# Hedgehog attention and a ReGLU feed-forward on one core: k and v of every batch in pairs of heads, a third output buffer, and a new order of work

## The chip, the cores and the metric

The kernel runs on one core of one Trainium2 chip. A core has a matrix engine (PE), whose weight loads are recorded apart (PEld); a vector engine (DVE); a scalar engine (ACT), which has the exponential; a general engine (POOL); and DMA engines, which take their work from queues that SP, POOL and ACT issue. Sums of PE land in eight PSUM banks of 128 x 512 words of 32 bits. The metric is the device time of one execution in microseconds, lower being better. The kernel before took 384.98 us (median of three runs: 384.98, 382.41 and 385.39).

## The reference

Attention with a feature map in place of the softmax (8 batches, 8 heads, 576 tokens, 64 dimensions, 128 features with both signs), whose output is laid out by token and fed to a gated feed-forward layer (4608 tokens, 512 wide, 1536 inside):

```python
def phi(x):                                   # x: (8, 8, 576, 64); w_phi: (64, 128)
    proj = np.einsum('bhsd,df->bhsf', x, w_phi)
    proj = proj - np.max(np.abs(proj), axis=-1, keepdims=True)
    return np.concatenate([np.exp(proj), np.exp(-proj)], axis=-1)
q_p, k_p = phi(q), phi(k)
kv  = np.einsum('bhsf,bhsd->bhfd', k_p, v)
z   = np.sum(k_p, axis=2)
num = np.einsum('bhsf,bhfd->bhsd', q_p, kv)
den = np.einsum('bhsf,bhf->bhs', q_p, z)[..., None] + 1e-06
x   = (num / den).transpose(0, 2, 1, 3).reshape(8 * 576, 512)
out = np.maximum(x @ w_gate, 0.0) * (x @ w_val) @ w_out
```

As written, `proj - max` is exponentiated with both signs, and the maximum is one number per token. The kernel therefore exponentiates the projection without it (exp(p) and exp(-p)) and brings exp(-max) and exp(max) in later, as factors of each token: on v for k (`ek`), and on the product for q (`cq`).

## The kernel before

**Atoms and their order.** The work of all eight batches is cut into some 1,400 pieces, the atoms. Each is a small function that issues a few instructions. They are registered in the order in which the program defines them, and they are run in the order of a string of numbers, `ORDER` (line 26). Nothing else sets the order: every engine, and every DMA queue, takes its instructions in the order in which the atoms issue them. A prime behind a number lets the atom choose the second of two engines (`copy_of`, for instance ACT in place of DVE for a copy). `zN` stands for filler: N matmuls of 512 columns on a tile of zeros, whose result nobody reads (`keep_busy`).

**Keys.** `kr` projects k with `w2` (w_phi twice, once in each half of the rows) in 64-row matmuls: the upper and lower half of PE's rows work on different heads or blocks, into two banks. For that k must stand with its 64 dimensions on the partitions. In batches 0 and 1 PE itself transposes k and q, and DVE or ACT copies the result out of PSUM (`tT`, `turned_copy`, line 284). From batch 2 on (`TURN = 2`) a transposing DMA on SP's queue does it (kT and qT, line 292). Then DVE takes the row maximum (line 319), ACT the two exponentials (`kp`, line 368) and the factors `ek`. POOL multiplies v by `ek` for both signs (`vs`, line 328), and the column behind them, a copy of `ek`, gives z.

**kv.** In batches 0 and 1, k and v are laid out in pairs of heads: the two heads of a pair have 2 x 576 tokens, laid on 128 partitions by 9, which makes 36 blocks of 128 rows for a batch, 64 rows of one head above 64 of the other. The blocks are worked in five or six items (`K_CUTS`), and `kv_pairs` (line 493) sums each half of the heads in 72 matmuls of 64 rows into two banks. Batches 2 to 7 take 512 tokens of each head in four blocks of 128 (four items of 8 blocks, one for each pair of heads), and the remaining 64 tokens of each head, the tails, in an item of their own for two batches at once: loads `km` and `vm`, a transposing DMA, a projection, and `vsm` (line 395), whose other half of the rows is zero. `kv_heads` (line 469) sums a pair of heads in 20 matmuls of 128 rows, 16 for the main tokens and 4 for the half-empty tails.

**Queries and the feed-forward.** q is projected in the same way, exponentiated on ACT (`qp`, line 565), and multiplied by kv (`n`, line 595). DVE puts the two signs together and divides (POOL or DVE for the last product, `xu`), and a DMA or PE transposes the result into `xT`, the input of the feed-forward layer. Its matmuls (`fv` and `fg`, line 725, four of 128 rows each; `fo`, line 773, twelve for a tile of 128 tokens) make the greater part of PE's work, and they are strewn between the small pieces of later batches' attention. A copy takes val out of PSUM (line 740), DVE makes h of it and the gate (line 747), a copy takes the output tile into one of two buffers `out_sb` (line 787), and a DMA on SP's queue stores it (line 754).

**Queues.** SP's queue carries v, the transposes and the stores; POOL's carries k, q and the weights, cast to bf16 on the way. A store that is issued behind a transpose waits for it on the queue.

## Time and profile before

| | |
|---|---|
| runs, us | 384.98, 382.41, 385.39 (median 384.98) |
| the profiled execution, us | 382.8, with a span of 380.8 |
| granted clock of PE | 1.00 |
| PE busy | 365.3 us, 96% of the span, 3452 matmuls |
| DVE, ACT, POOL busy | 290.4, 213.6, 151.2 us |
| feed-forward matmuls (lines 725 and 773) | 97.9 + 98.0 + 97.6 us of PE |
| kv in 128-row matmuls (line 486) | 480 |
| products of tails on POOL (line 395) | 12.3 us in 12 |
| stores of output | 32 of 256 KB, 2.9 us to landing |

The span runs from the first to the last recorded instruction; the time of the execution has 2.0 us around it. A group's row names the line, the engine and the operation, the tile written and those read, the shapes and the count; behind the bar stand its busy time and the mean of one, and behind the second bar the idle time of the engine ahead of these instructions, with what ended it. In a timeline row stand the start, the duration and the engine; brackets behind it hold a wait and what it waited for. A share of the chain that ended last says how much of the span had its cause on that engine or line.

### The profile page before, as it was taken

How to read it: one execution, taken by the hardware profiler on the slowest of the kernel's cores; microseconds unless marked ns; L12 is line 12 of the kernel's file. 1: busy time of each engine (PE TensorE's matmuls, PEld its weight loads, DVE VectorE, ACT ScalarE, POOL GpSimd, SP SyncE). 2: the span in 40 equal slices, each digit the busy share in tenths (PEclk: the TensorE clock that was granted, in tenths of full speed). 3: DMA queues.
4: the chain of work that ended last, by engine and by line, in shares of the span. 5: the costliest groups of instructions: out<-in, count | busy, mean ns of one | idle time of the engine just before them, and what ended most of it. 6: DMA issues, size and time to landing. Idle time of an engine off the chain costs nothing.

```text
span 380.8 us, 8916 instructions
## 1 busy us (share of the span) xinstructions
PE 365.3 (96%) x3452; PEld 196.8 (52%) x3502; DVE 290.4 (76%) x633; ACT 213.6 (56%) x509; POOL 151.2 (40%) x201
## 2 busy tenths in 40 slices
PE   7789999898999999999989999999999999999996
PEld 4467455445555545464545544465455444444443
DVE  6998989797886789888858886988768927834641
ACT  6997888776776556885864549882750212111101
POOL 5882663359265283911752035933710220010000
PEclk9999999999999999999999999999999999999999
DMA  8999999999199959880378768720410131011003
GB/s 258 204 200 218 228 143 143 199 239 118 36 208 228 161 87 167 164 183 14 72 126 197 108 162 126 144 16 16 109 58 2 28 87 53 3 53 71 2 0 110
DMA packets 87929, 45.10 MB, mean 118 GB/s; under 512 B 55824, under 2 KB 82000, under 8 KB 87888
## 3 DMA queue, kind: packets, MB, share of 16 engines
q1 hardware_dynamic: 60208, 30.42, 36.4%
q0 software_dynamic: 27200, 13.57, 28.2%
q10 hardware_dynamic: 480, 0.56, 0.5%
q8 instruction: 27, 0.44, 0.5%
q14 instruction: 14, 0.11, 0.1%
HBM read 37.78 MB, written 9.44 MB: 124 GB/s over the span
## 4 chain that ended last, share of the span: by engine, by line
PE 79%; ACT 8%; DMA 5%; POOL 2%; issue 2%; DVE 1%; SPq 1%; another core or an unknown queue 0%; DVEq 0%; POOLq 0%
PE pa L725 44%; PE pa L773 20%; PE pa L595 4%; PE pa L312 4%; PE pa L486 3%; ACT kp L368 3%; ACT qp L565 3%; DMA vn<-in_v_dram 3%; DMA out_dram<-out_sb 2%; PE pa L547 2%; POOL vs L328 1%; SPq L292 1%; PE pa L509 1%; PE pa L271 1%; DMA vn<-in_k_dram 1%
## 5 line engine op out<-in xcount | busy, mean ns | idle before, releaser
L725 PE MATMUL pa<-xT,wv_sb 128*128 128x512 bf16 (+1 forms) x384 | 97.9, 370 | 0.9
L725 PE MATMUL pa<-xT,wg_sb 128*128 128x512 bf16 (+1 forms) x385 | 98.0, 370 | 0.8
L773 PE MATMUL pa<-wo_sb,h 128*128 128x512 bf16 (+2 forms) x427 | 97.6, 373 | 1.1 <-issue 0.3
L747 DVE SCALAR_TENSOR_TENSOR h<-pa,val_sb 128x512 bf16<-128x512 f32 (+1 forms) x112 | 74.6, 669 | 26.8 <-PE pa L725 20.7
L740 ACT CAST val_sb<-pa 128x512 bf16<-128x512 f32 (+1 forms) x67 | 38.1, 575 | 97.9 <-PE pa L725 88.8
L635 POOL TENSOR_TENSOR xu<-u,r 128x512 bf16<-128x512 f32 x36 | 37.3, 1041 | 139.3 <-DVE r L633 69.7
L565 ACT ACTIVATE qp<-pa 128x512 bf16<-128x512 f32 x144 | 76.2, 616 | 14.4 <-PE pa L547 14.1
L368 ACT ACTIVATE kp<-pa 128x512 bf16<-128x512 f32 (+1 forms) x152 | 77.6, 603 | 11.8 <-PE pa L312 10.4
L328 POOL TENSOR_TENSOR vs<-vn,ek 128x512 bf16<-128x512 f32 (+1 forms) x68 | 67.4, 1004 | 34.4 <-DMA vn<-in_v_dram 18.0
L725 PEld LDWEIGHTS <-wv_sb 128*128 128x128 bf16 x448 | 41.8, 98 | 45.0 <-issue 1.2
L725 PEld LDWEIGHTS <-wg_sb 128*128 128x128 bf16 x448 | 41.6, 98 | 43.4 <-issue 0.5
L773 PEld LDWEIGHTS <-h 128*128 128x128 bf16 x444 | 40.8, 98 | 44.6 <-issue 0.8
L319 DVE TENSOR_REDUCE mq<-pa 128x4 f32<-128x512 f32 x72 | 46.5, 683 | 11.1 <-PE pa L312 11.0
L319 DVE TENSOR_REDUCE mk<-pa 128x4 f32<-128x512 f32 (+1 forms) x76 | 47.8, 654 | 3.9 <-ACT kp L368 2.3
L626 DVE TENSOR_TENSOR u<-pa,t 128x195 f32<-128x195 f32 (+3 forms) x120 | 38.1, 333 | 3.3
L614 DVE TENSOR_TENSOR t<-pa,cq 128x195 f32<-128x195 f32 (+3 forms) x120 | 36.9, 326 | 2.5 <-PE pa L595 1.3
L787 DVE COPY out_sb<-pa 128x512 f32<-128x512 f32 x21 | 14.5, 688 | 28.8 <-PE pa L773 20.3
L595 PEld LDWEIGHTS <-qp 128*128 128x128 bf16 x640 | 28.1, 98 | 14.2 <-ACT qp L565 0.9
L740 DVE CAST val_sb<-pa 128x512 bf16<-128x512 f32 (+1 forms) x45 | 30.7, 682 | 4.4 <-PE pa L725 3.0
L595 PE MATMUL pa<-kv,qp 128*128 128x65 bf16 x640 | 31.1, 193 | 1.1 <-ACT qp L565 0.5
L787 ACT COPY out_sb<-pa 128x512 f32<-128x512 f32 (+1 forms) x15 | 8.9, 594 | 23.5 <-PE pa L773 18.7
L486 PEld LDWEIGHTS <-kp 128*128 128x128 bf16 x480 | 16.7, 97 | 5.9 <-issue 1.5
(68 smaller groups left out, 262.7 us busy)
## 6 DMA issues: line engine op xcount, KB each, us to landing
out_dram<-out_sb SPq DMA_DIRECT2D x32, 256.0 KB, 2.9
vn<-in_v_dram SPq DMA_DIRECT2D x6, 1024.0 KB, 7.1
qn<-in_q_dram POOLq DMA_DIRECT2D x8, 512.0 KB, 8.5
kn<-in_k_dram POOLq DMA_DIRECT2D x6, 512.0 KB, 8.6
wv_sb<-in_moe_w_val_dram POOLq DMA_DIRECT2D x3, 512.0 KB, 10.4
wg_sb<-in_moe_w_gate_dram POOLq DMA_DIRECT2D x3, 512.0 KB, 9.1
wo_sb<-in_moe_w_out_dram POOLq DMA_DIRECT2D x1, 1536.0 KB, 19.9
vn<-in_v_dram SPq DMA_DIRECT2D x1, 1152.0 KB, 11.7
```

The lines of the kernel that those rows point to most:

```text
L319: nc.vector.tensor_reduce(m, some.rearrange("p (c f) -> p c f", f=F), axis=AX.X, op=ALU.max, apply_absolute_value=True,)
L328: eng.tensor_tensor(dst[:, :, s, 0:D], src, ek[:, :, s : s + 1].to_broadcast(list(src.shape)), op=ALU.mult,)
L368: nc.scalar.activation(st["kp"][:, s, 0 : n // 2, par, :], st["banks"][par][:, 0 : n // 2 * F].rearrange("p (a f) -> p a f", f=F), AF.Exp, ...
L565: nc.scalar.activation(x["qp"][:, s, slot].rearrange("p a b -> p (a b)"), st["cols", i][par], AF.Exp, scale=sign,)
L595: nc.tensor.matmul(pn[:, E * (2 * i + s) : E * (2 * i + s + 1)], lhsT=x["qp"][:, s, slot, blk, :], rhs=kv_of(b, lo + i)[:, s, :],)
L614: nc.vector.tensor_tensor(x["t", j][rows, 0:n], ab[:, :, 1], c[:, :, None].to_broadcast([np_, n, E]), op=ALU.mult,)
L626: nc.vector.tensor_tensor(x["u"][rows, lo : lo + n], ab[:, :, 0], x["t", j][rows, 0:n], op=ALU.add)
L635: copy_of(alt, nc.gpsimd, nc.vector).tensor_tensor(x["xu"], x["u"][:, :, 0:D], x["r"].to_broadcast([P, H, D]), op=ALU.mult)
L725: nc.tensor.matmul(ps, lhsT=w[:, dc, P * fi : P * fi + P], rhs=xTs[g][:, dc, lo:hi], start=(dc == 0), stop=(dc == NDC - 1),)
L740: copy_by(copy_of(alt, "ACT", "DVE"))(st["val", n], ps)
L747: nc.vector.scalar_tensor_tensor(st["h2"][:, fi, lo:hi], ps, 0.0, st["val", n], op0=ALU.max, op1=ALU.mult)
L773: nc.tensor.matmul(po, lhsT=st["h2"][:, fi, P * t : P * t + P], rhs=wo_sb[:, fi, c0:c1], start=(fi == 0), stop=(fi == NFC - 1),)
```

## The change

Batches 2 to 7 take the layout of batches 0 and 1. `load_k` and `load_v` call `load_pairs` for every batch; the transposing DMA of k covers 18 slices of 128 in place of 16, those of the tails go, and so do the loads `km` and `vm`, `k_tails`, `vsm`, the zeroed `vs_mix` and `kv_heads`. Every batch from 1 on has five items of k, of 8, 8, 8, 8 and 4 blocks, and two calls of `kv_pairs`. In numbers: PE does 1152 kv matmuls of 64 rows where it did 480 of 128 rows and 288 of 64. The exponentials of k go from 136 of 512 columns and 16 of 256 to 124 and 40. The pool of `kp` and `vs` has six buffers (five before, with the tails in another pool). `out_sb` has three buffers in place of two. `keep_busy` counts in halves: `z8` is four matmuls of 512 columns, `z1` one of 256; fillers are 15 of 512 and three of 256 columns where there were six of 512. The numbers of the atoms are others, so `ORDER` is another string throughout.

```diff
-ORDER = """7 z3 82 92 93 83' 84 87 94 86 8 0 98 102 85 89 90 91 88 103 z1 104 96 97 108 105 95 107 106 z1 112
+ORDER = """7 z8 49 59 60' 50 z1 51 53 61 63 55 8 64 1 52 0 69 70' z3 71 62 66 68 54 72 56 57' 58 z8 79 75 74
...
-    sb_k = ctx.enter_context(tc.tile_pool(name="sb_k", bufs=5))
+    sb_k = ctx.enter_context(tc.tile_pool(name="sb_k", bufs=6))
...
-    vs_mix = [singles.tile([P, H, 2, E], BF16, name=f"vsm{half}") for half in range(2)]
 
     def keep_busy(n):
-        scratch = bank()
-        for _ in range(n):
+        scratch = bank().rearrange("p (a b) -> p a b", b=P)
+        for i in range(0, n, 2):
+            wide = 2 * min(2, n - i)
             nc.tensor.matmul(
-                scratch.rearrange("p (a b) -> p a b", b=P),
+                scratch[:, 0:wide],
                 lhsT=zeros,
-                rhs=zeros[:, None, :].to_broadcast([P, 4, P]),
+                rhs=zeros[:, None, :].to_broadcast([P, wide, P]),
             )
...
     def load_k(b):
-        (load_pairs if b < TURN else load_main)(b, "kn", k, nc.gpsimd, BF16)
+        load_pairs(b, "kn", k, nc.gpsimd, BF16)
 
     def load_v(b):
-        (load_pairs if b < TURN else load_main)(b, "vn", v, nc.sync, FP32, buf=f"vn{b % 2}")
+        load_pairs(b, "vn", v, nc.sync, FP32, buf=f"vn{b % 2}")
...
     for i in range(B // 2):
-        if 2 * i >= TURN:
-            atoms.add("ld", f"km{i}")(lambda alt, i=i: load_tails(i, "km", k, nc.gpsimd, BF16))
-            atoms.add("ld", f"vm{i}")(lambda alt, i=i: load_tails(i, "vm", v, nc.sync, FP32))
...
-                t = inputs[f"{n}T", b] = sb_in.tile([P, H * C // 2, P], BF16, name=f"{n}T{b % 2}")
-                nc.sync.dma_start_transpose(
-                    out=t, in_=inputs[f"{n}n", b].rearrange("p h c d -> p (h c d)")
-                )
+                rows = inputs[f"{n}n", b]
+                if n == "q":
+                    rows = rows.rearrange("p h c d -> p (h c d)")
+                t = sb_in.tile([P, rows.shape[1] // P, P], BF16, name=f"{n}T{b % 2}")
+                inputs[f"{n}T", b] = t
+                nc.sync.dma_start_transpose(out=t, in_=rows)
...
-    for i in range(TURN // 2, B // 2):
-        atoms.add("turn", "km", i)(lambda alt, i=i: turn_tails("km", i))
...
-        if b >= TURN:
-            for u in range(NU):
-                st = k_item(
...
-                kv_heads(b, u, st)
-            return
-        cuts = [0] + K_CUTS[b] + [NB]
+        cuts = [0] + K_CUTS[min(b, 1)] + [NB]
...
-                None,
+                lambda lo=lo, hi=hi: inputs["kT", b][:, lo // 2 : hi // 2],
                 lambda lo=lo, hi=hi: v_blocks(lo, hi),
...
-                            out_sb = sb_g.tile([P, DM], FP32, name="out_sb", bufs=2)
+                            out_sb = sb_g.tile([P, DM], FP32, name="out_sb", bufs=3)
...
-    for half in range(2):
-        nc.vector.memset(vs_mix[half][SM * (1 - half) : SM * (2 - half)], 0.0)
```

Three places show how the instructions move. The lines of the changed kernel are some 60 to 80 lower where the same code stands further up (486 and 509 become 447, 754 becomes 690, 284 becomes 279).

The first is PE at the first kv block of batch 2. A row has the line, the operation, the tile written, and the tiles read; a number behind a name tells one buffer's use from the next, `kp` and `vs` are the exponentials of k and the scaled v of an item, `vsm0` the tails of v, and `pa` a PSUM bank. Before:

```order
L595 LDWEIGHTS qp_1526
L595 MATMUL pa_2019<-kv_1210,qp_1526 128x65
L486 LDWEIGHTS kp_1835
L486 MATMUL pa_2031<-vs_1832,kp_1835 128x65
...
L486 LDWEIGHTS kp_1681
L486 MATMUL pa_2031<-vsm0_102,kp_1681 128x65
```

and in the changed kernel:

```order
L307 LDWEIGHTS kT1_1566
L307 MATMUL pa_2027<-w2_100,kT1_1566 128x128
L447 LDWEIGHTS kp_1656
L447 MATMUL pa_2037<-vs_1791,kp_1656 128x65
L447 LDWEIGHTS kp_1656
L447 MATMUL pa_2038<-vs_1791,kp_1656 128x65
```

Before, 20 matmuls into one bank stand behind a 128-row product of q (line 595) and end with a tail's product after every four blocks. Now 72 matmuls into two banks in turn stand behind 64-row projections (line 307), and they need three items of the batch at once.

The second is ACT in the start, from the projections of the first queries to the first copies of val. `tT` is a transposed k or q, `xT` the input of the feed-forward layer, `x2` two such rows in a row. Before:

```order
L565 ACTIVATE qp<-pa 128x512 x2
L284 COPY tT_742<-pa 128x1024
L655 COPY xT<-pa 128x4x128 x2
L284 COPY tT_794<-pa 128x512
L368 ACTIVATE kp<-pa 128x4x128 x2
L740 CAST val_sb<-pa 128x256 x2
L655 COPY xT<-pa 128x4x128
```

and in the changed kernel:

```order
L503 ACTIVATE qp<-pa 128x512 x6
L279 COPY tT_756<-pa 128x512
L279 COPY tT_758<-pa 128x1024
L593 COPY xT<-pa 128x4x128
L279 COPY tT_794<-pa 128x1024
L363 ACTIVATE kp<-pa 128x4x128 x2
L676 CAST val_sb<-pa 128x256 x2
```

ACT has another copy of `tT` ahead of the first copy of `xT`, and the second copy of `xT` has gone to DVE.

The third is SP's queue at the end of batch 1 and the start of batch 2. A store's `out_sb` has the number of its buffer's use, `vn0` is v of batch 2, and the numbers behind `kT` and `qT` tell the batch's parity. Before:

```order
L292 DMA_TRANSPOSE qT0_1390<-qn_1388 128x16x128
L754 DMA out_0_dram<-out_sb_1484 128x512
L754 DMA out_0_dram<-out_sb_1596 128x512
L292 DMA_TRANSPOSE kT1_1607<-kn_1503 128x16x128
L214 DMA vn0_1635<-in_v_dram 128x8x256
L754 DMA out_0_dram<-out_sb_1668 128x512
L236 DMA vm_1685<-in_v_dram 64x8x64 x2
L298 DMA_TRANSPOSE qmT_1713<-qm_1710 128x4x128
L754 DMA out_0_dram<-out_sb_1776 128x512
```

and in the changed kernel:

```order
L291 DMA_TRANSPOSE qT0_1225<-qn_945 128x16x128
L690 DMA out_0_dram<-out_sb_1528 128x512
L218 DMA vn0_1536<-in_v_dram 128x4x576
L291 DMA_TRANSPOSE kT1_1566<-kn_1564 128x18x128
L690 DMA out_0_dram<-out_sb_1606 128x512
L690 DMA out_0_dram<-out_sb_1672 128x512
L690 DMA out_0_dram<-out_sb_1734 128x512
L295 DMA_TRANSPOSE qmT_1768<-qm_1740 128x4x128
```

The load of v has moved from behind the transpose of k3 and behind the second store to the place directly behind the first store. Three stores stand behind the transpose where there were two, and the tails' loads are gone.

151 lines of the change are left out of this document (55 added, 96 removed), and 33 rows, old and new, of the table ORDER.

## The prediction

> **What bounds the kernel now.** I read the page first, then the table of windows, then the chain.
>
> ```profile
> span 380.8 us, 8916 instructions
> PE 365.3 (96%) x3452; PEld 196.8 (52%) x3502; DVE 290.4 (76%) x633; ACT 213.6 (56%) x509; POOL 151.2 (40%) x201
> ...
> PE 79%; ACT 8%; DMA 5%; POOL 2%; issue 2%; DVE 1%; SPq 1%; another core or an unknown queue 0%; DVEq 0%; POOLq 0%
> ```
>
> PE is busy 96% of the span and makes 79% of the chain that ended last. Such a share is an average, so the next view asks where the other 15.5 us lie. Its columns are the stretch, its length, and the busy time (and count) of PE, PEld, DVE, ACT and POOL, then clock and DMA.
>
> ```profile
> 0.00:10.00 10.00, 7.82 (x37) 4.03 (x37) 6.43 (x13) 6.64 (x20) 5.06 (x14) 1.00 0.84 254
> 10.00:20.00 10.00, 7.70 (x160) 5.11 (x159) 9.78 (x20) 9.88 (x32) 9.04 (x14) 1.00 1.28 205
> 20.00:30.00 10.00, 8.55 (x196) 6.81 (x191) 9.63 (x34) 9.29 (x21) 8.55 (x12) 1.00 1.40 201
> ...
> 60.00:80.00 20.00, 18.65 (x177) 10.23 (x181) 17.32 (x45) 16.88 (x42) 6.38 (x7) 1.00 1.32 210
> 80.00:100.00 20.00, 18.99 (x230) 10.93 (x231) 16.97 (x36) 14.41 (x33) 15.61 (x22) 1.00 0.77 109
> 100.00:120.00 20.00, 19.84 (x196) 10.28 (x197) 15.12 (x35) 13.89 (x32) 13.57 (x17) 1.00 0.81 184
> ...
> 180.00:200.00 20.00, 18.85 (x202) 10.38 (x203) 14.09 (x30) 14.51 (x35) 12.77 (x16) 1.00 0.50 96
> ...
> 360.00:380.80 20.80, 17.08 (x91) 8.43 (x89) 7.12 (x11) 1.62 (x3) 0.00 (x0) 0.99 0.18 50
> ```
>
> Three stages show. Up to 30 us PE idles 5.9 us, while from 10 us on ACT and DVE are full (9.88 and 9.78 of 10): the start belongs to them. From 30 to 360 us PE has 19.84 of 20 almost everywhere, except 60 to 100 us (2.4 us idle) and 180 to 200 us (1.2 us). The last 3.7 us are the drain and the last store, which the change leaves as they are. So an edit moves the end in one of three ways only: by less PE work, by fewer PE waits in those stretches, or by the moment at which the feed-forward matmuls start. Time saved on POOL, ACT or DVE elsewhere counts for nothing.
>
> **Less PE work: the kv products.** Batches 2 to 7 now use the 64-row form that batches 0 and 1 use already, so the trace has both prices. These are rows of the chain:
>
> ```profile
> 21.47 1.28 PE pa L509 x72
> 47.44 1.09 PE pa L509 x72
> ...
> 106.24 2.59 PE pa L773 x12
> 112.94 0.61 PE pa L486 x20
> ```
>
> Removed: 6 batches x 4 units x 20 matmuls, 24 blocks of 0.61 us, 14.6 us. Added: 6 x 2 blocks of 72 matmuls, 12 x 1.09 = 13.1 us (the two halves of the rows run beside each other: 1.09 / 72 is 15 ns a matmul, against 30 ns for a whole one). That is 1.6 us less, because the half-empty products of the tails go. At the price of the start, 1.28, it is 15.4 us, 0.7 more: these are the ends; I take the 1.09, the price between feed-forward work, where the new blocks stand too. The k projections keep their number (216 weight loads of k from the transposing DMA before, 192 + 24; now 216).
>
> A change between 64-row and 128-row matmuls has a price of its own:
>
> ```profile
> 51.51 1.03 PE L725 MATMUL pa<-xT,wg_sb 128*128 128x512 bf16 x4
> 52.47 0.39 PE L547 MATMUL pa<-tT,w 64*128 64x512 bf16 x2
> ```
>
> Four matmuls at 2.59 / 12 = 0.216 us from 51.51 end their turn at 52.37, and the 64-row ones begin at 52.47: 0.10 us. I take the same for the way back. [...] Counted over PE's order, though, both kernels have 43 runs of 64-row matmuls and so 86 changes of mode: every new kv block stands against projections that are 64-row anyway. I put the changes of mode at nothing.
>
> The filler matmuls on zeros go from 6 to 18.
>
> ```profile
> L200 PE MATMUL pa<-zeros 128*128 128x512 bf16 x6 | 3.1, 583 | 1.0 <-DVE zeros L806 1.0
> ```
>
> At 3.1 / 6 = 0.52 us each, the nine added of 512 columns and three of 256 are 5.4 us, all ahead of the first feed-forward step. PE idles 4.5 us in the first 20 us, which is the cover; a group that outlasts it delays the projections behind it, and then ACT. I count 0 and keep 1 us for the range.
>
> **The start.** Up to the first feed-forward matmul the order holds the same work but for these copies, which change engine:
>
> ```profile
> L655 ACT COPY xT<-pa 128x512 bf16<-128x512 bf16 x7 | 4.3, 609 | 1.0 <-PE pa L271 1.0
> L284 ACT COPY tT<-pa 128x1024 bf16<-128x1024 bf16 x1 | 1.0, 1036 | 0.0
> L284 ACT CAST tT<-pa 128x512 bf16<-128x512 f32 x1 | 0.6, 624 | 0.0
> L284 ACT COPY tT<-pa 128x512 bf16<-128x512 bf16 x1 | 0.6, 586 | 0.0
> ...
> L284 ACT CAST tT<-pa 128x256 bf16<-128x256 f32 x1 | 0.4, 372 | 0.2 <-PE pa L271 0.2
> ...
> 28.91 0.60 PE L725 MATMUL pa<-xT,wv_sb 128*128 128x256 bf16 x4
> ```
>
> To the copy of xT that lets the matmul at 28.91 go, ACT now does 256 x2, cast 512 x2, copy 512 x2, 1024 x1 and xT x1 (0.74 + 1.25 + 1.17 + 1.04 + 0.61 = 4.81 us), where it did 256, 512, 1024 and xT x2 (0.37 + 0.62 + 1.04 + 1.22 = 3.25 us). That is 1.56 us more on the engine that is full; DVE loses about 2 us there and two memsets. ACT's idle time from 10 to 30 us is 0.83 us, so 0.7 to 1.6 us come later if ACT alone sets the pace, and up to 0.4 earlier if it was DVE. I take 0.8 later. PE then has nothing to fill in: a later start is a later end.
>
> **Waits that go.** PE's waits after the start, from its timeline:
>
> ```profile
> 70.65 0.38 PE L271 MATMUL pa<-ident,xu 128*128 128x128 bf16 x4 [1.09 <-DVE out_sb L787]
> ...
> 91.14 0.19 PE L486 MATMUL pa<-vsm,kp 128*128 128x65 bf16 x1 [0.56 <-POOL vsm L395]
> ...
> 92.08 0.28 PE L486 MATMUL pa<-vs,kp 128*128 128x65 bf16 x4 [0.29 <-POOL vs L328]
> ...
> 199.67 0.29 PE L486 MATMUL pa<-vs,kp 128*128 128x65 bf16 x4 [0.94 <-DVE out_sb L787]
> ```
>
> The first and last (2.0 us) are one story. DVE's copy into out_sb waits for an earlier store to free the buffer, the PSUM bank stays full, and PE wants it:
>
> ```profile
> DVE out_sb L787 <- DMA out_dram<-out_sb: 8.2, 3, 3.4
> ...
> 65.22 1.05 SPq L754 DMA_DIRECT2D out_dram<-out_sb  x2
> 66.35 3.95 SPq L292 DMA_TRANSPOSE kT<-kn  x1
> 70.41 0.52 SPq L214 DMA_DIRECT2D vn<-in_v_dram  x1
> 71.02 0.53 SPq L754 DMA_DIRECT2D out_dram<-out_sb  x1
> ```
>
> With three buffers the copy needs only the third store back. In the new order three stores stand behind the transpose of k3, but the fourth copy needs the store ahead of it, so the wait goes. It stays if stores lag by three as well: bounds 0 and 2.0, I take 2.0. What is late next there is the product of the transposes, which the order has well ahead of use.
>
> The other two (0.85 us) come from v of batch 2, which stands behind that transpose on SP's queue, and from the tails' vsm ahead of it on POOL:
>
> ```profile
> 80.08 1.04 POOL L328 TENSOR_TENSOR vs<-vn,ek 128x512 bf16<-128x512 f32 x1 [9.61 <-DMA vn<-in_v_dram]
> ...
> L328 POOL TENSOR_TENSOR vsm<-vm,ek 64x512 bf16<-64x512 f32 x12 | 12.3, 1049 | 3.3 <-DMA vm<-in_v_dram 3.0
> ```
>
> Now that load stands directly behind the first store, at about 63 us instead of 70.41, and the 12.3 us of vsm on POOL are gone. I take 0.85; it is 0 if the load lands no earlier.
>
> **Waits that come.** Batch 1 first, whose v releases POOL at 40.87:
>
> ```profile
> 40.87 0.61 POOL L328 TENSOR_TENSOR vs<-vn,ek 128x256 bf16<-128x256 f32 x1 [8.40 <-DMA vn<-in_v_dram]
> ...
> L414 POOL CAST vs<-ek 128x16 bf16<-128x16 f32 (+1 forms) x35 | 8.7, 247 | 0.0
> ```
>
> The kv block that the chain has at 47.44, 18.5 us after 28.91, now stands one feed-forward step (8 x 0.216) and 0.2 us of small work earlier, 16.6 us after a start at 29.7: at 46.3. POOL must by then have done four vs of 512, two of 256 and four small copies (4 x 1.04 + 2 x 0.61 + 4 x 0.25 = 6.4 us): 47.3, if v lands as before. PE waits up to 1.0 us, nothing if v lands 1.0 us earlier; I take 0.8. Batch 2: its five items of k now follow each other on ACT, 16 exponentials of 512, 4 of 256 and 8 for q within some 11.5 us of PE work; at 2.06 us for four
>
> ```profile
> 7.86 2.06 ACT L368 ACTIVATE kp<-pa 128x512 bf16<-128x512 f32 x4 [0.52 <-PE pa L312]
> ```
>
> the 24 long ones alone take 12.4 us, some 5 us too much with the rest. Eight PSUM banks let PE run ahead; behind the exponentials stand the copies of val, for which the gate products wait. Bounds 0 and 5, I take 0.8, as most of the backlog falls in banks that PE wants late.
>
> **The sum.** -1.6 (kv) + 0.8 (start) - 2.0 (out_sb) - 0.85 (v2, vsm) + 0.8 + 0.8 (new waits) = -2.05 us. The profiled execution took 382.8 us with a span of 380.8, which gives 380.75. The three runs have a median of 384.98 (382.41 to 385.39); from that it is 382.9. I forecast between them, **382.0 us**, a little faster. About 1% (3.85 us) is what a measurement of this kernel tells from no change.
>
> **Rivals.**
> - *All covers hold.* The kv work and the four waits go (-4.45), nothing new comes, and ACT's extra copies hide: 380.5 from the median, 378.4 from the profile; with the hidden rests of the 2.4 us idle at 60 to 100 us, 377. For it: POOL has 12.3 us less to do and SP three transposes less. Against it: ACT is full in the start. Faster by over 1%: chance 0.35.
> - *The third buffer doesn't do what it is there for.* Stores lag on SP behind transposes (3.95 us of issue at 66.35) by more than one tile; the 2.0 us stay, and the sum is 0: 383 to 385. Together with the forecast, within 1%: 0.50.
> - *kv waits for v (slower).* A kv block now needs three of a batch's five items at once, so one late v holds 72 matmuls and all that follows in PE's order. Place: batch 1, whose v is loaded while the weights are. It decides from a landing at 39.9 us on, each us later costs one. To pass the other gains and 1% it must land after about 46.5 us, or ACT's backlog cost its full 5 us: 389 to 391. For it: DMA is at its fullest until 55 us, and wo's load of that time took 19.9 us to land by the page. Against: v's own load took 11.7. Chance 0.15.
>
> ```profile
> wo_sb<-in_moe_w_out_dram POOLq DMA_DIRECT2D x1, 1536.0 KB, 19.9
> vn<-in_v_dram SPq DMA_DIRECT2D x1, 1152.0 KB, 11.7
> ```
>
> **Range.** From 377 (all covers hold) down to 376.5 for a faster start, up to 388.0, the forecast with kv at its dear price (+2.3), fillers (+1), and a backlog of 3 us; that leaves out most of the slower rival. Faster 0.35, within 1% 0.50, slower 0.15.
>
> **What would show it.** Blocks of 72 at 1.09 us in all batches; no wait of PE on out_sb; first feed-forward matmul at 29.7 us; POOL's first vs of batch 2 by about 73 us; a PE wait of under 1.2 us at batch 1's first kv block and about 1 us between 70 and 80 us. It is wrong if PE shows idle time over 1.5 us in any 20 us after 30, or if the feed-forward work starts before 28.5 or after 31 us.

## The result and the profile after

The changed kernel took 383.95 us in the median of 21 runs (380.50 to 385.21), the kernel before 380.66 us in 21 runs (379.71 to 385.86). The ratio is 1.0062, with a 95% interval of 1.0034 to 1.0091: 0.6% slower, where 0.8% faster was forecast. The three runs of before that stood ahead of the prediction (median 384.98) lay high; of the later ones most lie near 380.5. So the comparison goes by the ratio, and the account below by the two profiled executions: 382.8 us with a span of 380.8 before, 384.1 us with a span of 382.3 after, 1.5 us more. The profiled execution of before is not a typical one: it lies 2.1 us above its kernel's median. So most of its executions lose about 2 us less than its profile shows; at which place, no profile tells.

The page of the changed kernel first, the lines that answer to those shown of before:

```profile
span 382.3 us, 9719 instructions
PE 365.0 (95%) x3852; PEld 195.6 (51%) x3898; DVE 287.6 (75%) x635; ACT 216.9 (57%) x538; POOL 138.2 (36%) x190
```

Then its table of windows, with the columns as before (the last three are the granted clock, the share of the DMA engines, and GB/s):

```profile
0.00:10.00 10.00, 7.01 (x43) 3.43 (x43) 4.80 (x12) 7.22 (x22) 5.92 (x16) 1.00 0.84 252
10.00:20.00 10.00, 8.28 (x166) 5.50 (x166) 8.44 (x17) 10.00 (x32) 9.19 (x13) 1.00 1.28 205
20.00:30.00 10.00, 9.04 (x189) 6.92 (x190) 9.59 (x34) 10.00 (x23) 7.19 (x10) 1.00 1.34 185
...
40.00:60.00 20.00, 16.45 (x233) 8.79 (x232) 11.76 (x19) 13.60 (x33) 9.08 (x14) 0.91 1.16 166
60.00:80.00 20.00, 19.79 (x196) 11.01 (x198) 18.35 (x52) 15.42 (x41) 7.45 (x10) 1.00 0.69 135
80.00:100.00 20.00, 19.84 (x298) 11.10 (x301) 18.02 (x36) 16.42 (x40) 10.44 (x15) 1.00 1.12 184
...
180.00:200.00 20.00, 19.35 (x243) 10.27 (x245) 16.85 (x37) 15.29 (x41) 12.52 (x17) 1.00 0.80 114
200.00:220.00 20.00, 18.64 (x215) 10.23 (x218) 15.83 (x38) 11.91 (x26) 2.88 (x4) 1.00 0.46 91
```

The holes from 60 to 100 us, where PE had 18.65 and 18.99 of 20, are gone. Two new ones have come: 40 to 60 us, with 16.45 of 20 busy and a clock of 0.91, the only stretch of the table with less than 1.00; and around 200 us. PE's timeline says what they are:

```profile
28.33 0.60 PE L661 MATMUL pa<-xT,wv_sb 128*128 128x256 bf16 x4
...
46.41 0.36 PE L447 MATMUL pa<-vs,kp 64*128 64x65 bf16 x12 [1.34 <-POOL vs L323]
48.90 1.84 PE L447 MATMUL pa<-vs,kp 64*128 64x65 bf16 x60 [2.13 <-POOL vs L393]
...
58.37 1.26 PE L447 MATMUL pa<-vs,kp 64*128 64x65 bf16 x72
59.47 0.38 PE L307 MATMUL pa<-w,tT 64*128 64x128 bf16 x8
...
201.20 1.09 PE L447 MATMUL pa<-vs,kp 64*128 64x65 bf16 x60 [1.58 <-POOL vs L393]
...
368.03 10.55 PE L709 MATMUL pa<-wo_sb,h 128*128 128x512 bf16 x59
```

Batch 1's first kv block waits twice, 1.34 + 2.13 = 3.47 us, for the scaled v that POOL makes, and once it has all of it, its 60 matmuls take 1.84 us. On POOL's timeline stands why:

```profile
43.03 1.05 POOL L323 TENSOR_TENSOR vs<-vn,ek 128x512 bf16<-128x512 f32 x1 [9.03 <-DMA vn<-in_v_dram]
...
48.59 0.26 POOL L393 CAST vs<-ek 128x16 bf16<-128x16 f32 x1
```

POOL waited 9.03 us for v, which landed at 43.0 us (40.87 before), and then needed 5.8 us for the products. The kv block was ready to go at 45.07 us. The windows of half a microsecond from there show the second half of the loss, in the clock column:

```profile
48.00:48.50 0.50, 0.00 (x0) 0.00 (x0) 0.00 (x0) 0.00 (x0) 0.50 (x1) 1.00 1.68 187
48.50:49.00 0.50, 0.10 (x5) 0.10 (x6) 0.00 (x0) 0.00 (x0) 0.35 (x2) 0.65 0.88 130
49.00:49.50 0.50, 0.50 (x23) 0.50 (x24) 0.00 (x0) 0.00 (x0) 0.00 (x0) 0.50 1.23 198
...
51.50:52.00 0.50, 0.50 (x3) 0.20 (x3) 0.50 (x2) 0.37 (x1) 0.00 (x0) 0.50 1.22 197
52.00:52.50 0.50, 0.42 (x3) 0.25 (x3) 0.49 (x1) 0.50 (x2) 0.00 (x0) 0.94 1.20 189
```

From 48.65 to 52.05 us PE had half its clock, just when it had work again. By an estimate from that column this costs 0.35 x 0.5 + 6 x 0.25 + 0.06 x 0.5 = 1.7 us, or 1.6 without the first quarter of a microsecond, in which PE still waited.

**The account.** From the first feed-forward matmul to the last group of output matmuls it is 368.03 - 28.33 = 339.70 us after. Before it was 337.67, by the start at 28.91 and this row:

```profile
366.58 10.55 PE L773 MATMUL pa<-wo_sb,h 128*128 128x512 bf16 x59
```

So this part is 2.03 us longer. PE's waits of over 0.25 us in it are 5.05 us (1.34 + 2.13 + 1.58) against 2.88 (1.09 + 0.56 + 0.29 + 0.94), and the clock adds 1.7. What is left, 2.03 - 2.17 - 1.7 = -1.84 us, is less PE work (-1.7 with 1.6 us for the clock).

| term | forecast, us | profile, us |
|---|---|---|
| less PE work (kv) | -1.6 | -1.84 |
| start of the feed-forward work | +0.8 | -0.58 |
| waits on out_sb | -2.0 | -2.03 |
| waits on vsm and on v of batch 2 | -0.85 | -0.85 |
| batch 1's kv waits for v | +0.8 | +3.47 |
| the clock after that wait | 0 | +1.7 |
| ACT's backlog in batch 2 | +0.8 | 0 |
| batch 5's kv waits for POOL | not foreseen | +1.58 |
| the drain | 0 | +0.05 |
| sum | -2.05 | +1.5 |

The start has one value for each kernel here, and it varies: in the eight profiles with the same work on PE, ACT and the queues up to this point, the first feed-forward matmul comes between 28.33 and 30.04 us (median 28.6). So the 0.58 us between 28.91 and 28.33 can be chance.

The theory to test: batch 1's wait for v, and the clock that falls after it, turned a gain into a loss. The rivals: that the wait itself costs, but not the clock; that PE would only wait somewhere else; and, for the other terms, that the order of the stores and not the third buffer took the waits on out_sb away, and that the start is set by ACT's copies.

### The profile page after: what moved, and what is told of

The parts are those of the page before. It is cut to its first block, busy times and chain, and to the rows that moved or that the text cites. A ratio compares the mean times of both kernels' runs of the same rounds, so it can differ in the third digit from the quotient of the medians.

```text
span 382.3 us, 9719 instructions
## 1 busy us (share of the span) xinstructions
PE 365.0 (95%) x3852; PEld 195.6 (51%) x3898; DVE 287.6 (75%) x635; ACT 216.9 (57%) x538; POOL 138.2 (36%) x190
## 5 line engine op out<-in xcount | busy, mean ns | idle before, releaser
L323 POOL TENSOR_TENSOR vs<-vn,ek 128x512 bf16<-128x512 f32 (+1 forms) x76 | 71.3, 953 | 38.1 <-ACT ek L374 28.2
L363 ACT ACTIVATE kp<-pa 128x512 bf16<-128x512 f32 (+1 forms) x164 | 78.7, 579 | 6.6 <-PE pa L307 4.7
L552 DVE TENSOR_TENSOR t<-pa,cq 128x195 f32<-128x195 f32 (+3 forms) x120 | 38.0, 328 | 3.5 <-PE pa L533 2.6
L676 DVE CAST val_sb<-pa 128x512 bf16<-128x512 f32 x45 | 30.9, 687 | 12.2 <-PE pa L661 11.0
L723 ACT COPY out_sb<-pa 128x512 f32<-128x512 f32 (+1 forms) x17 | 9.9, 584 | 31.7 <-PE pa L709 29.7
L447 PE MATMUL pa<-vs,kp 64*128 64x65 bf16 x1152 | 21.0, 192 | 5.1 <-POOL vs L393 3.7
L723 DVE COPY out_sb<-pa 128x512 f32<-128x512 f32 x19 | 13.1, 688 | 16.3 <-PE pa L709 16.2
```

What stands on the lines that cost most here:

```text
L323: eng.tensor_tensor(dst[:, :, s, 0:D], src, ek[:, :, s : s + 1].to_broadcast(list(src.shape)), op=ALU.mult,)
L363: nc.scalar.activation(st["kp"][:, s, 0 : n // 2, par, :], st["banks"][par][:, 0 : n // 2 * F].rearrange("p (a f) -> p a f", f=F), AF.Exp, ...
L552: nc.vector.tensor_tensor(x["t", j][rows, 0:n], ab[:, :, 1], c[:, :, None].to_broadcast([np_, n, E]), op=ALU.mult,)
L676: copy_by(copy_of(alt, "ACT", "DVE"))(st["val", n], ps)
```

## The experiments

Each is the changed kernel with one edit, but for two that put several together. The numbers in the fragments of `ORDER` are atoms: 246 is batch 1's first kv block with its copies 247 and 248, 9 the load of v1, 45 the transpose of the q tails, 11 and 33 load and transpose of k2, 13 the load of q2, 4, 5 and 6 the last loads of the val, gate and output weights, 211 and 212 vs of batch 1's item 1, 749 and 750 vs of batch 5's last item, 709 the waiting xu.

**PE kept busy while it waits.**

```diff
-1118 290 294 246 292 252
+1118 290 294 z30 246 292 252
```

> The changed kernel with 15 more matmuls of 512 columns on zeros (15 x 0.216 = 3.2 us) directly ahead of the kv block that waits 1.34 + 2.13 us in batch 1. Theory (an idle PE loses its clock): the wait itself stays, since the same v and the same products on POOL end it, but PE is busy in it; its clock then stays at 1.00 where the changed kernel shows 0.66 and 0.50 from 48 to 52 us, the 60 kv matmuls take 0.9 us in place of 1.84, and the span falls by about 1.7 us, to 380.6. Rival (the clock falls for another reason, or costs nothing): the span stays at 382.3. If the fillers end after the products on POOL, it is up to 0.5 us longer.

382.66 us in the median of 12 runs, ratio 1.0042 (1.0013 to 1.0071). In the profiled execution v's load was issued 1.5 us later than in the changed kernel's and POOL began at 44.36 us, so the whole execution has to be read from the moment at which the block goes on:

```profile
50.22 1.08 PE L448 MATMUL pa<-vs,kp 64*128 64x65 bf16 x60 [1.40 <-POOL vs L394]
```

and the windows around it:

```profile
48.00:50.00 2.00, 0.82 (x15) 0.29 (x14) 0.00 (x0) 0.00 (x0) 2.00 (x5) 1.00 1.26 183
50.00:52.00 2.00, 1.78 (x71) 1.40 (x72) 0.44 (x1) 0.58 (x2) 0.17 (x1) 1.00 1.20 194
52.00:54.00 2.00, 1.95 (x10) 0.88 (x9) 1.84 (x4) 2.00 (x7) 0.94 (x1) 1.00 1.25 190
```

The clock stays at 1.00, and the 60 matmuls take 1.08 us in place of 1.84. From the block to the end of the span it is 381.9 - 50.2 = 331.7 us, where the changed kernel needs 382.3 - 48.9 = 333.4. Of these 1.7 us, 0.33 is a shorter wait in batch 5; 1.4 is the clock. The theory said 1.7. In none of the 12 runs was the mean clock under 0.998, in 15 of the changed kernel's 21 it was. Those 15 have a median of 384.3 us, the other six 381.6; that difference also holds the waits that go with a fall. A low mean alone doesn't tell of a loss: of the 126 runs of the kernel before that were taken beside these experiments, 55 had a mean under 0.998, with a median of 380.8 us, and the other 71 one of 380.3. The interval of the ratio overlaps that of the changed kernel (1.0034 to 1.0091), so the price of the clock is shown by the two profiles and not by the times.

**The block put behind two feed-forward steps.**

```diff
-294 246 292 252 256 254 248 296 300 200 34 201 1119' 247 1120 298 1121 258 328 332 260 251 255 253 1122 211
+294 292 252 256 254 296 300 200 34 201 1119' 1120 298 1121 258 328 332 260 251 255 253 1122 246 248 247 211
```

> The changed kernel with batch 1's first kv block and its two copies moved behind two feed-forward steps (the four half steps 12 and 13 of the first tile, 4 x 0.87 = 3.5 us, and four small projections). Theory (the place of the block costs wait and clock): no wait on POOL's vs is left there, the clock stays at 1.00, and the span falls by 3.5 + 1.7 = 5.2 us, to 377.1. Rival (ACT and DVE have to follow with the copies of val and with h, and the queries of batch 1 come later): a wait on val or on qp takes the place of a part, and the span falls by under 3 us.

382.46 us, ratio 1.0024 (0.9991 to 1.0057). The wait for POOL's vs is gone, as expected; but the span of the profiled execution is 382.7, for another stop came:

```profile
58.57 0.28 PE L308 MATMUL pa<-w,tT 64*128 64x128 bf16 x3 [2.29 <-issue]
```

In the middle of a group of eight matmuls PE stood still for 2.29 us and waited for nothing that the profile shows; the clock then fell to 0.50 until 62 us. From the first feed-forward matmul (29.36 us) to the last group (368.40) it is 339.04 us. Without the stop (2.29 + 0.22), one wait of 0.41 on qp and a clock loss of 1.7 it would be 334.4, and the theory's 5.2 us less than 339.70 is 334.5. So the sum fits in this one execution, with the stop taken out. The times don't bear it out: the theory's span of 377.1 would be a time of about 379, but eight of the 12 runs had a mean clock of 0.998 or more, and their median is 381.9, the fastest 381.7. What the stop is, in how many of the other runs it was, and what else holds them back stays open.

**v loaded earlier.**

```diff
-29 45 121 156
+29 9 45 121 156
...
-205 9 139
+205 139
```

> The changed kernel with the load of batch 1's v issued ahead of the transpose of the q tails on SP's queue, at about 20 us in place of 29.24. Theory (the late landing of v makes the wait): v lands by 36 us, POOL's products start at about 36 in place of 43.03, the kv block waits for nothing, the clock stays, and the span falls by up to 5.2 us, to 377.1; what the load takes from the weights' loads may bring the first feed-forward matmul from 28.3 to 29 or 30, which leaves 378 to 379. Rival (the DMA engines are full until 45 us, so v lands no earlier, or the weights land as much later): the span stays within 1 us of 382.3.

381.29 us, ratio 0.9990 (0.9961 to 1.0020), with an interval wholly below that of the changed kernel; the profiled span is 379.1. Both halves of the theory came out, and the price was higher than I had put it:

```profile
27.21 0.85 PE L267 MATMUL pa<-ident,qn 128*128 128x128 bf16 x8 [1.65 <-DMA qn<-in_q_dram]
```

and on POOL:

```profile
38.16 1.05 POOL L324 TENSOR_TENSOR vs<-vn,ek 128x512 bf16<-128x512 f32 x1 [1.53 <-ACT ek L375]
```

POOL now waits for ACT's factors and no longer for v, PE has no wait of over 0.25 us between 30 and 190 us, and the clock is 1.00 in all of that stretch but its first 0.9 us. But q of batch 1 lands later, PE waits 1.65 us for it, and the clock falls behind this wait, from 27.44 to 30.86 us:

```profile
27.00:27.50 0.50, 0.29 (x5) 0.30 (x6) 0.00 (x0) 0.00 (x0) 0.50 (x2) 0.94 1.23 205
27.50:28.00 0.50, 0.50 (x9) 0.50 (x7) 0.00 (x0) 0.00 (x0) 0.50 (x2) 0.50 1.28 212
```

The first feed-forward matmul comes at 30.94 us. The DMA share is 1.23 and 1.28 in these rows, so it looks as if the load of q lost what that of v won; that is argued from one profile.

**Two buffers of out_sb.**

```diff
-                            out_sb = sb_g.tile([P, DM], FP32, name="out_sb", bufs=3)
+                            out_sb = sb_g.tile([P, DM], FP32, name="out_sb", bufs=2)
```

> The changed kernel with two buffers of out_sb in place of three. Theory (the third buffer took the two waits on out_sb away): PE waits on out_sb again, as in the kernel before (1.09 and 0.94 us), in at least one place between 60 and 210 us, and the span grows by 1 to 2 us, to 383.3 to 384.3. Rival (the new order of the stores on SP's queue did it): no wait on out_sb, span 382.3.

The six runs have a median of 392.56 us. The ratio of 1.0217 (1.0152 to 1.0283) goes by the three fastest of them alone (387.45 to 391.0): 2.2% slower than before, with an interval that reaches below 2%, and 1.5% slower than with three. The profiled execution is one of the three longest (394.16), so it shows a price near the highest. PE's timeline has one row for it, and SP's queue the reason:

```profile
85.36 1.87 PE L661 MATMUL pa<-xT,wg_sb 128*128 128x512 bf16 x4 [7.12 <-DVE out_sb L723]
```

```profile
67.56 0.37 SPq L218 DMA_DIRECT2D vn<-in_v_dram  x1
78.81 2.46 SPq L291 DMA_TRANSPOSE kT<-kn  x1
81.31 4.35 SPq L690 DMA_DIRECT2D out_dram<-out_sb  x3
```

The transpose of k3 isn't issued before 78.81, one store stands ahead of it and three behind it. With three buffers the fourth copy into out_sb needs the store ahead of the transpose; with two it needs the first of those behind it. PE waits 7.12 us and then works at 0.50 of its clock for 4.7 us, until 90.04. So the third buffer is no gain of 2 us on top of the new order: without it even the fastest run is 3.5 us over the changed kernel's median. What the buffer would do in the old order wasn't run.

**q2 and the transpose of k2 moved back.**

```diff
-148 11 33 181 186
+148 11 181 186
...
-6 293 13 1105
+6 293 1105
...
-230 232 231' 217
+230 232 231' 13 33 217
```

> The changed kernel with the load of q of batch 2 (POOL's queue, issued at 33.10) and the transpose of k of batch 2 (SP's queue, issued from 34.04 on) moved behind batch 1's products on POOL, as the kernel before has them later too (52.39 and 42.92). Theory (v of batch 1 lands late because these two share the DMA engines with it): v lands about 2 us earlier, near the 40.9 us of the kernel before, the wait of PE at batch 1's kv falls from 3.5 to about 1.5 us, the clock falls less, and the span goes from 382.3 to between 379 and 380.5. Rival (the weights' loads hold v back, not these): v lands at 43 us as before and the span stays at 382.3. A new wait is possible: the first projections of k of batch 2 stand at 69.0 us, and would wait if the transpose lands later than that.

383.90 us, ratio 1.0063 (1.0029 to 1.0097), like the changed kernel; POOL began at 43.00 us. The edit did only half of what it says: the load of q2 went back, but SP's queue has nothing between the load of v1 and the transpose of k2, so that it was issued at 34.38 as before, whatever its place in `ORDER`. It clears the load of q2.

**Batch 5's products ahead of the waiting xu.**

```diff
-739 709 758 710 737 762 760 764 766 749 738 736 740 768 750
+739 749 750 709 758 710 737 762 760 764 766 738 736 740 768
```

> The changed kernel with the two products vs of batch 5's last item (256 columns) ahead of the product xu of batch 4 that waits on POOL until 196.61 us for a transpose to release its buffer. Theory (the wait of 1.58 us of PE at 201.20 is POOL's queue: work that was ready at 186.6 us stands behind the waiting xu): the two products run before 190 us, those of the next item start at 197.6 in place of 198.9, and PE's wait falls to about 0.3 us, the span by 1.3, to 381.0. Rival (the wait comes from the factors ek, which ACT gives at 196.5): the wait stays at 1.58.

The profiled span is 381.0, as forecast, with this row in place of 201.20:

```profile
199.91 1.09 PE L448 MATMUL pa<-vs,kp 64*128 64x65 bf16 x60 [0.19 <-POOL vs L394]
```

In the changed kernel POOL's row ahead of these products was

```profile
196.61 1.04 POOL L573 TENSOR_TENSOR xu<-u,r 128x512 bf16<-128x512 f32 x1 [6.10 <-DMA xT<-xu]
```

So the wait was POOL's queue: work that could have run stood behind an instruction that waited for a DMA. In the median it hardly shows: 383.30 us, ratio 1.0060 (1.0032 to 1.0088). Nine of the 12 runs had a mean clock under 0.998, about the share of the changed kernel. Taken apart, these nine have a median of 383.5 us (384.3 there) and the other three 380.4 (381.6 there), so a gain of about 1 us is likely, on few runs.

**Two copies of the start back on DVE.**

```diff
-194' 250'
+194 250
```

> The changed kernel with two copies of the transposed k and q of batch 1 in the start (512 and 1024 columns) on DVE in place of ACT. The prediction's step (ACT sets the start, each us of copies more is a later start): without these 0.6 + 1.0 us on ACT the first feed-forward matmul comes up to 0.8 us earlier than 28.33, and the span falls as much. Rival (DVE sets the start as much as ACT does): it comes at 28.3 or up to 0.8 us later.

383.97 us, ratio 1.0058 (1.0021 to 1.0094); the first feed-forward matmul at 29.58 us in place of 28.33. That speaks against ACT as the pace, but PE also waited 1.04 us for the load of q of batch 0 there (0.58 in the changed kernel), and the start varies by up to 1.7 us from one profile to the next, as said above. It is inconclusive.

**No fillers.**

```diff
-7 z8 49 59 60' 50 z1 51 53
+7 49 59 60' 50 51 53
...
```

> The changed kernel without any of the 18 matmuls on zeros. The prediction's step (they lie in PE's idle time and cost nothing): the first feed-forward matmul at 28.3 and the span as it is, within 0.5 us. Rival 1 (they hold up the projections behind them): up to 1 us earlier. Rival 2 (they keep PE's clock up in the start, as the fillers in batch 1's wait did: clock 1.00 in place of 0.50 to 0.66): clocks under 1.00 in the first 20 us, and a start that comes 0.5 to 3 us later.

380.23 us, ratio 1.0000 (0.9975 to 1.0025): all of the loss is gone, which none of the three cases had. The clock of the first 20 us is 1.00 without them, so they don't hold it up there. The first feed-forward matmul is at 29.12 us, within the 28.33 to 30.04 seen with the fillers:

```profile
29.12 0.60 PE L662 MATMUL pa<-xT,wv_sb 128*128 128x256 bf16 x4
...
47.53 1.09 PE L448 MATMUL pa<-vs,kp 64*128 64x65 bf16 x60 [1.48 <-POOL vs L394]
...
363.99 10.55 PE L710 MATMUL pa<-wo_sb,h 128*128 128x512 bf16 x60
```

The kv block thus stands later than in the changed kernel's profile, v landed at 41.66 us in this execution, and the wait is 1.48 us in place of 3.47, after which the clock did not fall. Only one of the 12 runs has a mean clock under 0.998. That the fillers cost the 0.6% is shown by the times, whose intervals don't overlap; by what way isn't. An earlier start with fillers would only make the wait longer where v's landing is fixed; but v also landed 1.4 us earlier here, and in the run with three edits below, also without fillers, it landed at 44.9. The account holds here too: 337.67 - 2.88 - 1.84, and the waits of 1.48 and 0.32, make 334.75 us; 363.99 - 29.12 is 334.87.

**Load and transpose of k2 behind the weights.**

```diff
-148 11 33 181 186
+148 181 186
...
-1103 4 1104 197 6 293
+1103 4 1104 197 11 33 6 293
```

> The changed kernel with the load of k of batch 2 (POOL's queue, 27.09 us) and its transpose moved behind the last load of the weights of val, so that it is issued at about 32 us and the transpose cannot start before some 42 us (34.04 in the changed kernel, 42.92 in the kernel before). Theory (the transpose of k2, which took SP's queue from 34.04 to 47.5, takes DMA time from the load of v): v lands at about 41 us in place of 43, PE's wait at batch 1's kv falls from 3.5 to 1.5 us, the clock stays at 1.00, and the span falls by 2 + 1.7 us, to about 378.6. Rival (v shares with the weights, which now come earlier, and not with the transpose): v lands at 43 us or later, span 382 or more.

380.09 us, ratio 0.9988 (0.9960 to 1.0015), 0.7% faster than the changed kernel. v landed at 41.7 us and POOL began there:

```profile
41.78 1.04 POOL L324 TENSOR_TENSOR vs<-vn,ek 128x512 bf16<-128x512 f32 x1 [6.73 <-DMA vn<-in_v_dram]
```

The profiled execution is the one of 12 whose mean clock was under 0.998 (383.05 us), and tells something of the clock. PE waited once in batch 1, 2.13 us until 47.64, and these are the windows behind the wait:

```profile
48.00:48.50 0.50, 0.50 (x45) 0.50 (x39) 0.00 (x0) 0.00 (x0) 0.00 (x0) 1.00 1.31 219
48.50:49.00 0.50, 0.50 (x25) 0.33 (x17) 0.01 (x1) 0.23 (x1) 0.00 (x0) 0.94 1.22 204
49.00:49.50 0.50, 0.50 (x3) 0.13 (x2) 0.50 (x1) 0.33 (x2) 0.00 (x0) 0.50 1.21 196
```

The clock fell 1.3 us after PE had gone back to work.

**One product put back on POOL.**

```diff
-210 212 1107
+210 1107
...
-230 232 231' 217
+230 232 231' 212 217
```

> The changed kernel with one product on POOL put back: the second half of vs of batch 1's item 1 and its copy (1.05 + 0.25 us), which the waiting kv block does not need (it takes items 2 to 4), goes behind the products of items 2 to 4. Theory (the wait is the landing of v plus POOL's 5.85 us of products ahead of the block): the block's last wait ends 1.3 us earlier, 47.55 in place of 48.85 for v at 43.03, the clock falls less or not at all, and the span falls by 1.3 to 3 us. Rival (another product or ek ends the wait): the span stays at 382.3.

381.43 us, ratio 1.0015 (0.9988 to 1.0042). In the profiled execution v landed at 43.2 us, and the block went on at 47.94, 4.7 us later (5.9 in the changed kernel):

```profile
47.94 1.09 PE L448 MATMUL pa<-vs,kp 64*128 64x65 bf16 x60 [2.13 <-POOL vs L394]
```

The wait is the landing plus POOL's work ahead of the block, as the theory has it: 1.2 us less work, 1.2 us less wait. The clock fell here too, from 48.9 us on. Two of the 11 runs compared had a mean clock under 0.998; a twelfth took 2130.18 us, at a clock of 1.00, and isn't in the ratio; its cause is not known.

**Put together.** The third is without fillers, with both edits on POOL; the fourth has load and transpose of k2 moved as well.

> The changed kernel without the matmuls on zeros, with batch 5's last item ahead of the waiting xu on POOL, and with batch 1's product put back as in the run with that alone. Theory: without the fillers the first feed-forward matmul comes at 29.1 us, batch 1's kv stands at 45.7, and with v at 41.7 to 43 and 4.55 us of products on POOL it waits 0.5 to 1.9 us with the clock at 1.00; no wait of over 0.3 us at batch 5. Span 377 to 378.5, the time 1.5 to 3 us under the kernel before. Rival (the gains overlap with the run without fillers): 378.3.

> The same three edits and the later load and transpose of k of batch 2. Theory: v lands at about 41 us, batch 1's kv waits under 0.5 us, span 376.5 to 377.5. Rival (the transpose does not matter for v): as the run with three edits, within 0.5 us; if the transpose of k2 comes too late for the projections at 69 us, longer.

Three edits: 378.91 us, ratio 0.9957 (0.9922 to 0.9993). Four: 378.31 us, ratio 0.9941 (0.9918 to 0.9963), 0.6% faster than the kernel before and 1.2% faster than the changed one. The profiled execution of the fourth:

```profile
40.01 1.04 POOL L324 TENSOR_TENSOR vs<-vn,ek 128x512 bf16<-128x512 f32 x1 [4.70 <-ACT ek L375]
```

```profile
28.89 0.60 PE L662 MATMUL pa<-xT,wv_sb 128*128 128x256 bf16 x4
...
45.47 1.25 PE L448 MATMUL pa<-vs,kp 64*128 64x65 bf16 x72
...
361.87 10.55 PE L710 MATMUL pa<-wo_sb,h 128*128 128x512 bf16 x59
```

v had landed before ACT had the factors for POOL, batch 1's 72 matmuls run through, and no wait of PE over 0.25 us is left behind the start. From 28.89 to 361.87 it is 332.98 us; the account says 337.67 - 2.88 - 1.84 = 332.95. So the less PE work of 1.84 us is real, and in these profiles the waits and the clock are all that had hidden it. Against the profiled execution of before this one is 4.9 us faster (377.94 and 382.8), by the medians beside it the gain is 2.1 us (378.31 and 380.38): again most executions of the kernel before lose less than its profile shows.

**What makes v late.** Two runs were to tell the four transfers beside v's load apart. The first holds back the transpose of k2 alone, with a small copy on SP's queue that waits for a factor of batch 1; its atom, 33, also goes behind 230 in `ORDER`.

```diff
+                if (n, b) == ("k", 2):
+                    gate2 = singles.tile([1, 1], FP32, name="gate2")
+                    nc.sync.dma_start(out=gate2, in_=inputs["ek", (1, 3)][0:1, 0:1, 0])
```

> The changed kernel with only the transpose of k of batch 2 held back: a copy of one number of batch 1's factors ek, which ACT gives at about 43.2 us, stands ahead of it on SP's queue; the load of k2 stays at 27.09 us and the weights' loads keep their places. Theory (the transpose takes DMA time from the load of v): v lands at about 41 us, as with the later load and transpose (41.6), the wait at batch 1's kv falls to 1.5 to 2.1 us, and the time comes out near 380.1, as there. Rival (the load of k2, or the later weights that it puts back, held v up): v lands at 42.5 to 43.5 us as in the changed kernel, and the time is near 384.

381.02 us, ratio 1.0017 (0.9980 to 1.0054). The transpose went out 11.7 us later, and v still landed at 43.2:

```profile
45.72 7.89 SPq L295 DMA_TRANSPOSE kT<-kn  x1
```

```profile
43.38 1.05 POOL L327 TENSOR_TENSOR vs<-vn,ek 128x512 bf16<-128x512 f32 x1 [7.65 <-DMA vn<-in_v_dram]
```

The second loads the weights as early as the kernel before.

```diff
-119 108 131 29 45 121 156 132 112 161 113' 158 114 142 143 3 144
+119 108 131 29 45 121 156 132 112 161 113' 158 114 142 143 3 5 4 144
...
-189 5 288
+189 288
...
-1103 4 1104
+1103 1104
```

> The changed kernel with the last load of the gate weights and the last of the val weights (512 KB each as they land) issued at about 22.5 and 23.3 us on POOL's queue, as the kernel before does (22.30 to 23.81), in place of 27.90 and 31.29. Theory (v of batch 1 shares the DMA engines with these two loads, which the changed kernel issues beside it): v lands at about 41 us in place of 43 to 43.4, PE's wait at batch 1's kv is about 1.5 us, the clock stays in most executions, and the time is near 380. Rival (the load of k of batch 2 holds v up, wherever the weights stand): v lands at 43 us, time near 384. The transpose of q of batch 1 and the first feed-forward matmul may come later, since the weights then share with the loads of the start.

384.75 us, ratio 1.0108 (1.0081 to 1.0134), the slowest but for two buffers. POOL began at 43.35 us; k2's transpose, whose k landed later now, was issued at 42.60, and that didn't help either. So in none of these profiles does taking away the transpose, the two weight loads or q2 alone bring v in earlier. For the transpose the times say something else: the median of 381.02 us is nearer to the theory's 380.1 than to the rival's 384, and the profiled execution (382.80) is longer than seven of the other 11. It is not cleared. What is left is the load of k2, issued at 27.09, just ahead of v's at 29.24. With it later v landed at 41.7, and with the three other edits too at 37.6, where the three alone had 44.9 in their profiled execution. In the ten profiles that have the fillers and k2's load at its place, and v's at its own, POOL began between 42.95 and 44.36 us, so the late landing in the changed kernel is no single accident. But the kernel before loads k2 at the same time (27.01) and had v at 40.87, and the run without fillers had it at 41.66 with k2's load where it was. So that load is at best a part of the cause, and the rest stays open: there is one profile of each kernel, and v's landing differs by more than 3 us between the two without fillers that have the same loads (41.5 and 44.9).

## Why the prediction was wrong

The step that failed is the one under "Waits that come": "nothing if v lands 1.0 us earlier; I take 0.8". It had the place, the mechanism and POOL's work right (6.4 us said, 5.8 measured), and assumed that v would land as before. v landed 2.1 us later, the block was ready 1.2 us earlier (45.07 us, 46.3 said), PE waited 3.47 us, and the clock, which the prediction left out, took 1.7 more: 5.2 us where 0.8 stood. The times bear out that this wait is the loss: with v earlier, with k2's load later, and without fillers, the interval of the ratio lies wholly below 1.0034, where that of the changed kernel begins. The slower rival, "kv waits for v", describes it and its rule was right: from a landing at 39.9 us on each microsecond costs one, and at 43.0 that gives 3.1. It had a chance of 0.15, on the ground that v's load took 11.7 us before; I hadn't asked what the new order issues beside that load, though the excerpt of a queue was at hand. It was also priced as though it had to eat all other gains and more (389 to 391), where the gains stayed and the sum came out at +1.5. Both signs that the prediction names for being wrong came: 3.55 us of idle time in one stretch of 20 (40 to 60 us), and a start of 28.33, ahead of 28.5.

Point by point:

- *kv*: right. 72 matmuls take 1.10 us from 58.37 to 59.47, the work that is left out 1.7 to 1.84 us in the account (1.6 said), confirmed by the runs without fillers and with four edits. The changes of mode, 86 in both kernels by the prediction's count, added nothing that could be seen in that sum (-1.84 us, -1.6 said).
- *out_sb*: the waits went as said (2.03), but for more than the reason given. In the new order the third buffer is worth up to 7.12 us of wait and a fall of the clock, not 2.0; "bounds 0 and 2.0" was wrong as bounds, since it priced the buffer in the old order. The rival that the buffer does nothing was wrong.
- *v of batch 2 and vsm*: the 0.85 us went. The moments were wrong: v's load was issued at 66.92, not at 63, and POOL's first product came at 78.77, not by 73, but PE had no wait there.
- *The start*: 28.33 us where 29.7 was said, and in eight profiles 28.33 to 30.04 with a median of 28.6, so a delay of 0.8 us isn't what they show; that the start became earlier than 28.91 isn't shown either. ACT is full as expected (10.00 of 10 twice), and still the copy of xT didn't come later in the changed kernel's profile. Why wasn't settled.
- *Fillers*: "I count 0" was wrong in a way I hadn't thought of. Without them the whole loss is gone; that they act through the start and batch 1's wait is argued, and v's landing may have a part in it.
- *ACT's backlog in batch 2*: no trace of it; PE has 19.79 and 19.84 of 20 from 60 to 100 us.
- *Batch 5*: not foreseen; a row of POOL's order would have shown it, ready products behind an xu that waits for a DMA.

## What to carry to other kernels

When a change brings one consumer forward, look first at what it consumes last, and at everything that the new order puts beside the transfer it needs: an earlier start in front of a fixed arrival is only a longer wait. A wait of PE has a second price, the clock behind it: after a wait of 2.13 us it was halved for 3.4 us, which cost up to 1.7 us here, and with matmuls in the greater part of the wait, where PE stood still for 1.40 us, it wasn't. And a buffer is worth what the order asks of it, so price it in the new order, by the stores that stand behind the longest stop of their queue.

## What the runs showed of the hardware

The granted clock knows two values in these traces, 1.00 and 0.50; a value between them in a window of half a microsecond is the edge of a fall. A fall lasted 3.4 us (48.65 to 52.05 us in the changed kernel) or twice that, 6.8 us (83.2 to 90.0 us with two buffers, 48.3 to 55.1 with the weights early). It came in all ten profiled executions in which PE waited 2.12 or 2.13 us for the last products of batch 1, with between 0 and 1.82 us of another wait shortly ahead, after the stop of 2.29 us, after a wait of 1.65 us for q, and in the wait of 7.12 us with two buffers. It didn't come after waits of 1.40 and 1.48 us in batch 1, nor after one of 1.89 us in batch 5 (with the weights early). So the length of the wait alone doesn't decide. Nor is the fall tied to the wait's end: around batch 1's wait it came between 0.9 us ahead of the end and 1.3 us behind it. What decides on it isn't shown; 1.65 us without work were enough for q (v loaded earlier), and 2.13 us where PE waited only once in batch 1 (k2 behind the weights).

How often the mean clock is low differs between kernels: it was under 0.998 in 15 of 21 executions of the changed kernel and in one of 12 without fillers. It explains at best a part of the spread of the kernel before, whose three runs ahead of the prediction had a median of 384.98 us and the 21 with them 380.66: of its 126 runs beside the experiments 29 took over 382 us, 20 of them with a mean under 0.998 and nine without, while 35 with such a mean took less. The rest stays open, and a median of three runs tells little under such a spread.
